# 122-token chunks, 32-bit transposes, Q in token order, one store per block, and a new job order in a convolution + token-mixing kernel

## The chip, the core and the metric

The kernel runs on one core of one Trainium2 chip. The metric is the device time of one execution in microseconds (us), taken several times; medians with the range are given. Every ratio between two kernels is the mean time of one kernel's fast runs over the mean time of the other's fast runs of the same rounds, so it is not quite the ratio of the medians quoted beside it. A run is "slow" when it is more than 1.5% above the fastest of its kernel. A profiled execution has a span of its own; it lies about 1.5 to 2 us under the timed figure of the same run.

In the profile, PE is the matmul engine, PEld its weight loads, DVE the vector engine, ACT the scalar engine, POOL the third compute engine (here it mostly issues the loads of x), and SP the engine that issues weight loads and output stores. "L640" is a line of that kernel's source.

## The reference

Eight batches of 4224 tokens with 192 features. A depthwise causal convolution over 7 taps with softmaxed weights per head, then a linear token mixer, a ReLU, and an output projection:

```python
# x: (8, 4224, 192) float32, weight: (8 heads, 7 taps), w_q/w_k: (192, 64), w_out: (192, 192)
w = softmax(weight)                                   # over the taps
out = einsum('hk,bskhg->bshg', w, windows of 7 tokens of x)   # y
# mixer
wq = y @ w_q
wk = y @ w_k
W_tok = (1/sqrt(64)) * einsum('bsd,btd->bst', wq, wk)
mixed = einsum('bst,btd->bsd', W_tok, y)
return (maximum(mixed, 0) @ w_out).astype(float32)
```

There is no softmax in the mixer, so `mixed = wq @ (wk.T @ y)`, and `wk.T @ y` is `w_k.T @ (y.T @ y)`. Both kernels use this. They form G = y.T y (192x192), then M = w_k.T G, then Z = relu(M.T q) and O = Z w_out, with two half sequences side by side in the 128 rows.

## The kernel before

Each batch goes through these jobs. **Y** is the convolution: a matmul with a band matrix over chunks of tokens, evacuated to bf16. **T** is the DVE transpose of y in 32x32 blocks. **Q** is the matmul of the transposed y with w_q. **G** accumulates y.T y, and **M** follows from it. **Z** and **O** follow, then the stores. A greedy list scheduler in the kernel source places all jobs in one order per engine, before anything runs. It takes each job's priority from `KEYS` and each duration from a small model.

```python
KEYS = {   # job kind: (start, length) in batches; priority of a job
    "Y": (-0.27, 0.38), "T": (0.24, 1.17), "Q": (0.01, 0.95), "G": (0.03, 0.98),
    "Z": (0.61, 1.2), "O": (1.24, 0.87),
}
CW, NCK = 120, 18           # 18 chunks of 120 tokens for each half; a chunk's load has 126 rows
...
# T: 6 transposes a batch, each of 128 x 1152 bf16 elements
(YB[:, g, c : c + 3, :].rearrange("p c d -> p (c d)"),
 Y[:, b % 2, 3 * k : 3 * k + 3, :].rearrange("p c d -> p (c d)"))
...
# Q: moving operand contiguous, output in a chunk-wise order that needs small extra casts
rhs = YB[r, g, :, 32 * blk : 32 * blk + 32]
...
# O: stores, each half of a block apart; q == 1 is the block's second part
for h in range(2):
    if rem:                                            # the last 64 tokens of each half
        parts = [(0, 64, row(h, 17 * CW), [[D, 64], [1, D]])]
    elif i < 3:
        parts = [(0, 128, row(h, 32 * i), [[CW * D, 16]] + chunk)]
    else:
        parts = [(0, 96, ...), (96, 126, ...), (126, 128, ...)]
    for p0, p1, at, dims in parts:
        st = P.dma("sp", lambda e, ...: e.dma_start(bass.AP(out_t, at, dims), src), og[orr], evs)
...
# POOL: batch 0 is loaded first; then the w_k and w_out casts, which wait for their weights;
# only after them the loads of batches 1 to 7, six batch buffers in all
```

## Time and profile before

| quantity | value | where it is read |
|---|---|---|
| time | 187.51 us (187.36 to 187.66, 3 runs) | timing |
| span of the profiled run | 185.6 us | page |
| first band matmul (job Y) | 13.70 us | timeline of PE |
| first Q matmul of batch 0 / batch 1 | 22.90 / 38.77 us | starts of L466 |
| period in the middle | 38.6 us for two batches, 19.3 each | starts of L466: 59.01 and 97.59 |
| transposes | 48, 62.6 us of DVE | groups |
| last compute / end | 174.7 / 185.6 us | timeline |

The first fence is from the page of the kernel before: the span in 40 slices of 4.64 us. Digits are tenths (9 is 90% or more); "PEclk" is the granted matmul clock; "DMA" is the mean busy share of the 16 DMA engines, and the last row is what they moved.

```profile
span 185.6 us, 4685 instructions
...
PE   7907977998998999979989999799899999799500
...
PEclk9995799999999999999999999999999999999965
DMA  3997999999999999999999999968634860588894
GB/s 58 139 200 81 119 186 186 190 184 209 279 332 282 250 252 315 280 188 274 325 309 206 263 309 308 177 199 302 193 100 126 263 206 15 170 266 253 272 313 129
```

PE is near full in the middle but falls to 7 or 8 tenths again and again, every three to five slices, so about twice in the 38.6 us of two batches. The clock is at half in the fourth slice (0.50 from 15 to 20 us), after PE had been idle in the third (busy for 1.30 us from 10 to 15 us). The DMA engines are full until about 120 us, except in the fourth slice (81 GB/s): POOL's casts had waited for the w_out weights until 13.6 us, and the loads of batch 1 stand behind these casts, the first issued at 17.0 us.

Two groups of the kernel before (line, engine, operation, output<-input, shapes, count | busy us, mean ns of one | idle before):

```profile
L780 DVE STREAM_TRANSPOSE yb<-y 128x1152 bf16<-128x1152 bf16 x48 | 62.6, 1349 | 0.4
...
L466 PE MATMUL ps<-yb,wq 32*64 32x288 bf16 x768 | 15.1, 285 | 1.2 <-DVE zt L787 0.6
```

A transpose of 1152 16-bit elements takes 1.30 us of DVE when they run back to back (62.6 us for 48; the mean of 1349 ns counts their overlap), six times a batch.

A stretch of the chain of work that ended last (start us, us, what), kernel before, one batch in the middle:

```profile
71.21 0.38 PE ps L403 x2
71.59 0.67 DVE zt L787
72.26 3.80 DVE yb L780 x3
76.09 0.32 DVE y L812
76.45 0.69 DVE zt L787
77.17 3.90 DVE yb L780 x3
81.07 0.59 DVE zt L787
```

Two runs of three transposes in a row, 3.8 and 3.9 us, stand in the chain here, with single evacuations between them. In this stretch the chain is on the vector engine, not on PE. Over 60 to 100 us, DVE transposes are 19.3% of the chain.

Windows of the middle, kernel before (stretch, its length, then busy us and count of PE, PEld, DVE, ACT and POOL, granted clock, DMA share, GB/s; the DMA share sums the packets' times over 16 engines and can pass 1 where packets overlap):

```profile
60.00:80.00 20.00, 19.77 (x260) 14.23 (x260) 17.43 (x28) 17.90 (x36) 5.50 (x7) 1.00 1.36 268
80.00:100.00 20.00, 18.30 (x234) 12.14 (x231) 17.37 (x31) 16.89 (x33) 0.00 (x0) 1.00 1.36 269
```

PE counts as busy for 38.1 of 40 us. Ends of matmuls are modelled, so this says less than it seems to: the prediction worked out from the columns that a batch needs 17.0 of its 19.3 us. (Its 2.4 GHz is what the trace of the changed kernel shows at full clock: matmuls start 82 ns apart with 192 columns and 215 ns apart with 512, so 320 more columns take 133 ns, 2.4 a nanosecond.)

### The profile page before, as it was taken

How to read it: one execution, taken by the hardware profiler on the slowest of the kernel's cores; microseconds unless marked ns; L12 is line 12 of the kernel's file. 1: busy time of each engine (PE TensorE's matmuls, PEld its weight loads, DVE VectorE, ACT ScalarE, POOL GpSimd, SP SyncE). 2: the span in 40 equal slices, each digit the busy share in tenths (PEclk: the TensorE clock that was granted, in tenths of full speed). 3: DMA queues.
4: the chain of work that ended last, by engine and by line, in shares of the span. 5: the costliest groups of instructions: out<-in, count | busy, mean ns of one | idle time of the engine just before them, and what ended most of it. 6: DMA issues, size and time to landing. Idle time of an engine off the chain costs nothing.

```text
span 185.6 us, 4685 instructions
## 1 busy us (share of the span) xinstructions
PE 158.1 (85%) x1934; PEld 105.7 (57%) x1934; DVE 141.1 (76%) x239; ACT 136.5 (74%) x261; POOL 49.2 (27%) x74
## 2 busy tenths in 40 slices
PE   7907977998998999979989999799899999799500
PEld 2303663576556765857477758574578567657300
DVE  4846786998699779985998689968995899767100
ACT  2114739985998789868997899769986998599600
POOL 6808999999207226000000000000000000000000
PEclk9995799999999999999999999999999999999965
DMA  3997999999999999999999999968634860588894
GB/s 58 139 200 81 119 186 186 190 184 209 279 332 282 250 252 315 280 188 274 325 309 206 263 309 308 177 199 302 193 100 126 263 206 15 170 266 253 272 313 129
DMA packets 53589, 40.39 MB, mean 218 GB/s; under 512 B 44096, under 2 KB 45376, under 8 KB 53568
## 3 DMA queue, kind: packets, MB, share of 16 engines
q0 software_dynamic: 41216, 13.64, 63.3%
q1 hardware_dynamic: 12352, 26.45, 43.9%
q8 instruction: 15, 0.25, 0.5%
q14 instruction: 6, 0.05, 0.1%
HBM read 27.73 MB, written 25.95 MB: 289 GB/s over the span
## 4 chain that ended last, share of the span: by engine, by line
PE 42%; DVE 25%; ACT 18%; DMA 6%; issue 2%; POOL 1%; ACTq 0%
DVE yb L780 19%; PE ps L623 9%; PE ps L403 7%; PE ps L625 7%; PE ps L466 6%; DMA xw<-in_x_dram 6%; ACT o_sb L782 6%; ACT zt L785 5%; ACT y L782 5%; PE ps L586 3%; DVE zt L787 3%; PE ps L517 2%; PE ps L518 2%; PE ps L601 2%; ACT qt L782 2%
## 5 line engine op out<-in xcount | busy, mean ns | idle before, releaser
L780 DVE STREAM_TRANSPOSE yb<-y 128x1152 bf16<-128x1152 bf16 x48 | 62.6, 1349 | 0.4
L782 ACT COPY o_sb<-ps 128x768 f32<-128x768 f32 (+1 forms) x66 | 51.7, 800 | 9.0 <-PE ps L625 4.8
L782 ACT CAST y<-ps 128x864 bf16<-128x864 f32 (+3 forms) x80 | 43.1, 631 | 7.3 <-PE ps L403 7.2
L623 PE MATMUL ps<-wall,zt 128*128 128x192 bf16 x272 | 45.5, 249 | 2.4 <-ACT y L782 1.4
L625 PE MATMUL ps<-wall,zt 128*128 128x384 bf16 x136 | 44.3, 326 | 0.0
L403 PE MATMUL ps<-xw,band 126*128 126x432 bf16 x128 | 33.2, 367 | 4.9 <-DMA xw<-in_x_dram 4.6
L205 POOL DMA_DIRECT2D xw<-in_x_dram x32 | 32.1, 1008 | 17.4 <-issue 17.4
L623 PEld LDWEIGHTS ps<-wall,zt 128*128 128x128 bf16 x272 | 26.5, 114 | 15.7 <-ACT y L782 4.4
L517 PE MATMUL ps<-y 128*128 128x192 bf16 x144 | 33.8, 248 | 1.2 <-DVE y L782 1.2
L518 PE MATMUL ps<-y 128*128 128x192 bf16 x144 | 33.7, 248 | 0.0
L787 DVE TENSOR_SCALAR zt<-ps 128x512 bf16<-128x512 f32 (+1 forms) x61 | 30.2, 522 | 4.1 <-PE ps L586 2.0
L785 ACT ACTIVATE zt<-ps 128x512 bf16<-128x512 f32 (+1 forms) x59 | 33.1, 609 | 0.0
L519 PE MATMUL ps<-y 128*128 128x128 bf16 x144 | 31.7, 220 | 0.0
L586 PE MATMUL ps<-qt,m_sb 128*128 128x512 bf16 (+1 forms) x80 | 25.6, 343 | 0.4 <-ACT qt L782 0.4
L782 ACT CAST qt<-ps 128x64 bf16<-128x64 f32 (+4 forms) x43 | 14.3, 400 | 11.9 <-PE ps L466 11.6
L782 DVE CAST y<-ps 128x864 bf16<-128x864 f32 x16 | 16.8, 1057 | 4.3 <-PE ps L403 3.6
L403 PEld LDWEIGHTS ps<-xw,band 126*128 126x128 bf16 x128 | 10.7, 102 | 15.9 <-issue 8.8
L518 PEld LDWEIGHTS ps<-y 128*128 128x128 bf16 x144 | 14.2, 99 | 5.2 <-issue 0.2
L517 PEld LDWEIGHTS ps<-y 128*128 128x128 bf16 x144 | 14.2, 98 | 4.9 <-DVE y L782 1.9
L601 PE MATMUL ps<-qt,m_sb 128*128 128x512 bf16 (+1 forms) x40 | 13.8, 344 | 3.6 <-DVE zt L787 3.1
L466 PE MATMUL ps<-yb,wq 32*64 32x288 bf16 x768 | 15.1, 285 | 1.2 <-DVE zt L787 0.6
L625 PEld LDWEIGHTS ps<-wall,zt 128*128 128x128 bf16 x136 | 15.3, 112 | 0.0
(64 smaller groups left out, 121.5 us busy)
## 6 DMA issues: line engine op xcount, KB each, us to landing
out_dram<-o_sb SPq DMA_DIRECT2D x48, 384.0 KB
xw<-in_x_dram POOLq DMA_DIRECT2D x24, 378.0 KB, 22.5
out_dram<-o_sb SPq DMA_DIRECT2D x16, 288.0 KB
xw<-in_x_dram POOLq DMA_DIRECT2D x8, 425.2 KB, 22.7
out_dram<-o_sb SPq DMA_DIRECT2D x16, 90.0 KB
out_dram<-o_sb SPq DMA_DIRECT2D x16, 48.0 KB
xw<-in_x_dram POOLq DMA_DIRECT2D x16, 29.2 KB, 26.6
xw<-in_x_dram POOLq DMA_DIRECT2D x8, 45.0 KB, 16.9
```

The costliest lines, as they stand in the source:

```text
L205: return e.dma_start(XW[0:rows, b % NX, slot : slot + n, :], bass.AP(x_t, base, [[D, rows], [CW * D, n], [1, D]]),)
L403: last = e.matmul(PS[:, k + j, 0:432], BAND[0 : 6 + CW, h, :], rhs, start=True, stop=True)
L517: e.matmul(PS[:, 7, 0:192], y[:, 0:128], y[:, 0:192], start=c == 0, **fl)
L518: e.matmul(PS[:, 7, 192:384], y[:, 256:384], y[:, 192:384], start=False, **fl)
L519: return e.matmul(PS[:, 7, 384:512], y[:, 128:256], y[:, 128:256], start=False, **fl)
L586: return e.matmul(PS[:, bk, 0:w], M_SB[:, b % 2, 256 * h : 256 * h + 128], QT[:, b % 2, s0 : s0 + w], start=True, stop=True)
L623: e.matmul(o[:, 192 * h : 192 * h + 192], ZT[:, zr, h, cols], WO1, start=h == 0, stop=False, **kw)
L625: last = e.matmul(o[:, 0:384], ZT[:, zr, 2, cols], WO2, start=False, stop=True, **kw)
L780: last = e.transpose(o, i)
L782: last = e.copy(o, i) if eng == "act" else e.tensor_copy(o, i)
L785: last = e.activation(o, i, AF.Relu)
L787: last = e.tensor_scalar(o, i, 0.0, None, op0=ALU.max)
```

## The change

Its intent, part by part:

1. Transposes of 32-bit pairs: two bf16 features are moved as one int32, so each of the 48 transposes has 576 elements instead of 1152. The Q matmul picks the even or odd features by a step of two.
2. Q in token order: each chunk's output goes straight to its token place, and the small casts go.
3. One store per block (both halves), so 40 stores; the last two full blocks are stored in two parts each. The remainder of 64 tokens of each half becomes one store; the kernel before had two of 64 rows.
4. Chunks of 122 tokens in loads of 128 rows; batch 0 in four groups, the first without waiting for a memset; the w_k and w_out loads wait for batch 0's second group; the weight casts are moved from POOL to DVE and ACT.
5. A recalibrated model and new priorities for the job order, and redundant semaphore waits are removed.

```diff
 KEYS = {
-    "Y": (-0.27, 0.38), "T": (0.24, 1.17), "Q": (0.01, 0.95), "G": (0.03, 0.98),
-    "Z": (0.61, 1.2), "O": (1.24, 0.87),
+    "Y": (-1.0, 0.64), "Q": (-0.3, 1.4), "G": (0.06, 0.63), "Z": (0.73, 1.5), "O": (1.59, 0.9),
 }
+CLOCK = {
+    "x0": (5.0, 6.6, 9.2, 11.6), "band": 6.5, "wq": 6.5, "wk": 11.0, "wo": 12.0, "x": (12.0, 12.0),
+    "store": 5.0, "now": 0.05, "hold": 1.5,
+}
...  (removal of redundant waits cut)
-    CW = 120
+    CW = 122
...
+    GROUPS = [[(0, 3), (3, 9), (9, 15), (15, 18)]] + [[(0, 9), (9, 18)]] * (B - 1)
...
     for s, (src, wd) in enumerate(((wk_t, DH), (wo_t, D))):
-        wload(2 * s, 0, 128, src, 0, wd, wl[s + 1])
+        wload(2 * s, 0, 128, src, 0, wd, wl[s + 1], [xg[0][1]])
...  (band matrix set-up, casts of the weights cut)
             return [(
-                YB[:, g, c : c + 3, :].rearrange("p c d -> p (c d)"),
-                Y[:, b % 2, 3 * k : 3 * k + 3, :].rearrange("p c d -> p (c d)"),
+                YB[:, g, c : c + 3, :].rearrange("p c d -> p (c d)").bitcast(I32),
+                Y[:, b % 2, 3 * k : 3 * k + 3, :].rearrange("p c d -> p (c d)").bitcast(I32),
             )]
...
-                        blk = j if h == 0 else (8 + j if j < 4 else 2 + j)
-                        rhs = YB[r, g, :, 32 * blk : 32 * blk + 32]
+                        c = 64 * ((0, 1, 2), (4, 5, 3))[h][j // 2] + j % 2
+                        rhs = YB[r, g, :, c : c + 63 : 2]
...  (Z and M jobs cut)
-            for h in range(2):
-                if rem:
-                    parts = [(0, 64, row(h, 17 * CW), [[D, 64], [1, D]])]
-                elif i < 3:
...
+            at = (b * S + 512 * i) * D
+            if rem:
+                src, dims = OUT[:, orr, 0, 0:D], [[HALF * D, 2], [D, 64], [1, D]]
+            elif tail:                                 # tail = b == B - 1 and i >= 2
+                at += 2 * q * D
+                src = OUT[:, orr, :, 2 * D * q : 2 * D * q + 2 * D]
+                dims = [[4 * D, 128], [HALF * D, 2], [1, 2 * D]]
+            else:
+                src = OUT[:, orr, :, :]
+                dims = [[4 * D, 128], [HALF * D, 2], [1, 4 * D]]
+            st = P.dma(
+                "sp", lambda e: e.dma_start(bass.AP(out_t, at, dims), src), og[orr], evs,
+            )
...  (the scheduler's cost model cut)
```

## The prediction

> **What bounds the kernel now.** 187.5 us timed, 185.6 us in the profile.
> - Head: the chain of waits has the first band matmul at 13.7 us, released by the landing of batch 0's first loads (issued by 3.3 us). The band matrix itself was ready at 9.9 us (timeline).
> - Middle: the chain repeats every two batches in 38.6 us, so 19.3 us per batch. Matmul columns at 2.4 GHz need 17.0 us of that; 2.4 us are stalls. They sit where PE waits for DVE and ACT results. DVE carries six transposes of 1.30 us per batch (62.6 us in all, 19% of the chain), and the two evacuating engines together about 33.5 us per batch, 87% of their time.
> - Tail: the last compute ends at 174.7 us. SP still issues stores until 183.3 us (23 issues in 18.9 us, 0.8 us each); 11 us follow the last matmuls.
>
> **Costs of the change.**
> 1. Transposes: 576 elements of 32 bits instead of 1152 of 16. The trace shows 1.04 ns per element plus about 0.1. [...]I estimate 0.65-0.7 us: -3.8 us of DVE per batch.
> 2. Q in token order: the small casts (8 to 64 columns, 0.15-0.22 us each) go; about -0.6 us of evacuation. Evacuation falls to some 29 us per batch, 14.5 per engine. Risk: Q's moving operand now has a step of two elements.
> 3. PE columns hardly change: an estimate of 137.5 us for the whole program, 17.2 us per batch with array-mode switches. PE becomes the limit of the middle. I expect 17.5-18 us per batch: about -11 us over the middle.
> 4. Head: the first load waits for no memset, three chunks land first, the shift chain shrinks (five predicated copies 2.75 us -> about 1.3). First band matmul near 7.5-8.5 us, -5.5 us. PE ran at half clock from 15 to 20 us (windows) after its idle gap; that penalty should also go. Some 5 us of idle stay while batch 0 lands and its chain Y-G-M fills.
> 5. Stores: 112 issues become 40[...]; the last two blocks are stored in halves. Bytes are the same. The last two batches of output come in about 19 us of PE time, 6.5 MB, near the 293-333 GB/s that stores alone reached, so a backlog of 1-2 MB stays: tail 4-6 us, saving about 6.
> 6. Loads: pure x loads ran at 187 GB/s written; row count falls 2%. Together loads and stores need about 17.5 us per batch when mixed. So DMA is close behind PE, and some waits for x are possible.
>
> **Sum.** 8 + 137.5 + 10 stalls (fill, drain, middle) + 5 tail = 160.5 in the profile, plus 1.9 = about 163 us. Range 156 to 172. Faster 0.97, same 0.02, slower 0.01.
>
> **What would show it.** Right: transposes 0.65-0.7 us; first band matmul before 9 us; batch period 17.2-18 us; DVE and ACT under 85% busy mid-run; last compute by 157, span end within 6 us of it; granted clock never 0.5 after the start. Wrong in step 1: transposes above 1 us; step 2: Q's 48 matmuls above 0.95 us; step 4: first matmul still released by the load or later than 10 us; step 5: SP issues until well past the last compute; step 6: PE waits released by x landings after 40 us.
>
> **What would make it wrong.** The job order comes from a model: engines work in order, so one mis-modelled time stalls PE each batch. DMA saturation: output starts later and faster, and stores of the remainder in [2,64,192] form may run on few engines.

The sum: 160.5 us in the profile and 163 us timed. What its steps take from the trace of the kernel before:

- Step 1: DVE casts of 512 and 864 elements took 691 and 1057 ns (medians), 1.04 ns per element, and a transpose of 1152 elements at 1.30 us is that plus about 0.1 us. That a 32-bit element takes no longer than a 16-bit one was the assumption: this trace has only 16-bit transposes.
- Step 3, the array-mode switches: in the middle (55 to 100 us) the start of a 128*128 matmul of 128 columns is followed by the next start after 55 ns, and after 149 to 170 ns when the next is one of Q's 32*64 matmuls.
- Step 6: the 17.5 us are the estimate. It fits the trace: 40.39 MB over eight batches are 5.05 MB a batch, which take 17.5 us at 289 GB/s, and the trace has 285 GB/s from 70 to 80 us and 290 from 90 to 100.

## The result and the profile after

The changed kernel took **177.91 us** (median of 4 runs, 177.14 to 179.23) against 187.58 us (187.36 to 188.32, 4 runs) of the kernel before. The ratio of the fast runs is 0.950 (95% interval 0.945 to 0.956). It is faster by 5%. The predicted 163 us and the range of 156 to 172 us missed it. The profiled run below (span 177.5 us) is the 179.23 us run, the longest of the four, and counts as fast.

The same rows of the page, kernel after, slices of 4.44 us:

```profile
PE   7739869999999999999999999999599999999300
...
PEclk9965978999999999999999999999969999999975
DMA  3999999999999999999999999555640585497980
GB/s 57 130 170 189 206 189 192 190 194 190 261 285 293 262 213 335 250 327 213 329 248 331 216 333 304 199 187 198 219 178 11 215 317 187 158 392 230 388 292 23
```

Three things are new. PE is at 9 tenths in every slice from the 7th to the 28th, without the dips of before. In slice 29 (124 to 129 us) it falls to half, and the clock follows in slice 30. The DMA engines have been at half since slice 26 (111 us), and in slice 31 they move 11 GB/s. So the hole falls in a time when the DMA engines are not full. (The 11 GB/s come after it and are not its sign: the kernel before has a slice of 15 GB/s, and e1 below one of 22.) At the end PE has nothing to do in the last two slices, and in the very last the DMA engines move only 23 GB/s.

The group of transposes after:

```profile
L787 DVE STREAM_TRANSPOSE yb<-y 128x576 int32<-128x576 int32 x48 | 33.8, 749 | 2.7 <-ACT y L795 2.7
```

The transposes cost 33.8 us, not 62.6. Back to back one takes 0.70 us (33.8 us for 48), so step 1 of the prediction held.

Windows of the middle, and of the stretch with the hole, kernel after, columns as before:

```profile
60.00:80.00 20.00, 19.63 (x257) 14.44 (x258) 13.57 (x27) 18.84 (x32) 0.00 (x0) 1.00 1.30 288
80.00:100.00 20.00, 19.59 (x255) 14.29 (x257) 14.88 (x29) 18.73 (x34) 0.00 (x0) 1.00 1.34 274
120.00:130.00 10.00, 7.56 (x116) 5.13 (x122) 6.58 (x14) 7.42 (x13) 0.00 (x0) 1.00 0.65 232
130.00:140.00 10.00, 9.69 (x116) 7.06 (x102) 5.34 (x10) 7.74 (x16) 0.00 (x0) 0.83 0.17 62
```

PE has 39.2 of 40 us in the middle. From 120 to 130 us it has only 7.6 of 10, and from 130 to 140 us the clock is 0.83. The chain over 60 to 100 us is now PE work almost throughout. The period is 17.83 to 17.95 us per batch (Q starts at 66.75, 84.70, 102.53 and 120.38 us), inside the predicted 17.5 to 18.

The chain at the hole, kernel after:

```profile
126.59 0.69 DVE zt L793
127.28 1.36 DVE yb L787 x2
128.73 0.53 PE ps L433 x2
```

and the waits of PE after 36 us, kernel after (what waited <- for what: us in total, times, longest):

```profile
PE ps L433 <- DVE yb L787: 2.2, 1, 2.2
```

The profile puts the hole down to a transpose, which is an inference: a wait for several semaphores is given to the one that came last. In the trace, L433 waits for two, one of DVE and one of the last x load. PE's sequencer passed the wait for x at 128.63 to 128.68 us and started the matmul at 128.73. The transpose that ended at 128.63 is simply next on an engine that kept working. That the load is the cause is shown by its landing, here, and by e1, e2 and e4 below. Its semaphore counts one update for each of 16 DMA engines and each of its DMAs, and this is when the last ten of the 48 updates came (us from the start of the span):

```
last load of x (batch 7, second half): kernel after
110.1 110.3 111.0 111.2 | 120.1 125.3 126.9 127.2 128.3 128.6
```

Forty-two updates had come by 111.2 us. Six, so two engines times three DMAs, came 9 to 17 us later. The x queue as a whole shows the same: it moved 58.8 GB/s from 105 to 110 us, then 9.8, 8.9, 5.9 and 7.9 GB/s in the next four stretches of 5 us, with about one row in flight on average.

The tail, kernel before and then kernel after:

```profile
175.00:186.00 11.00, 0.00 (x0) 0.00 (x0) 0.00 (x0) 0.00 (x0) 0.00 (x0) 0.63 0.70 229
```

```profile
165.00:170.00 5.00, 0.68 (x7) 0.36 (x4) 0.36 (x1) 1.40 (x2) 0.00 (x0) 1.00 1.03 383
170.00:178.00 8.00, 0.00 (x0) 0.00 (x0) 0.00 (x0) 0.00 (x0) 0.00 (x0) 0.56 0.33 110
```

Last compute ended at 166.4 us and the span at 177.5, an 11.1 us tail, where the prediction had 5. After 170 us only 110 GB/s moved, at a third of the DMA engines' time. The store completions in the trace show which part is late. The last part of the last full block has 14 engines done by 172.5 us and its last two updates at 173.7 and 174.8; the remainder store, issued at 169.1 us, has one update at 170.7 and its last two at 176.6 and 177.0 us, when nothing else was left.

The head, kernel after (timeline of PE: start, us, engine, line and operation, count, [idle before <-releaser]):

```profile
8.58 0.55 PE L433 MATMUL ps<-xw,band 128*128 128x144 bf16 x6 [1.10 <-ACT band L371]
9.86 0.30 PE L433 MATMUL ps<-xw,band 128*128 128x144 bf16 x2 [0.73 <-ACT y L789]
12.36 1.60 PE L433 MATMUL ps<-xw,band 128*128 128x288 bf16 x6 [2.20 <-DMA xw<-in_x_dram]
```

The first band matmul starts at 8.58 us, released by the band matrix and not by the load, as predicted. But PE then waits 2.2 us for batch 0's second group, the clock is 0.55 from 10 to 15 us, and another wait of 2.0 us follows at 21.6 us, where the casts of w_out wait for weights that landed only at 21.9 us:

```profile
ACT wo L789 <- DMA wst<-in_moe_w_out_dram: 1.7, 1, 1.7
```

### The profile page after: what moved, and what is told of

It is laid out like the page before. It is cut to its first block, busy times and chain, and to the rows that moved or that the text cites. A ratio compares the mean times of both kernels' runs of the same rounds, so it can differ in the third digit from the quotient of the medians.

```text
span 177.5 us, 4686 instructions
## 1 busy us (share of the span) xinstructions
PE 152.8 (86%) x1958; PEld 112.8 (64%) x1980; DVE 113.1 (64%) x228; ACT 138.1 (78%) x255; POOL 47.6 (27%) x71
## 3 DMA queue, kind: packets, MB, share of 16 engines
HBM read 27.77 MB, written 25.95 MB: 303 GB/s over the span
## 4 chain that ended last, share of the span: by engine, by line
PE 71%; DMA 8%; ACT 7%; issue 3%; POOL 2%; SPq 1%; DVE 1%; ACTq 0%; POOLq 0%
PE ps L640 13%; PE ps L433 11%; PE ps L642 11%; PE ps L597 9%; PE ps L498 8%; PE ps L526 7%; PE ps L527 6%; DMA xw<-in_x_dram 4%; DMA wst<-in_moe_w_out_dram 4%; PE ps L528 4%; POOL xw L252 2%; ACT qt L789 2%; ACT y L789 2%; SPq L310 1%; ACT o_sb L789 1%
## 5 line engine op out<-in xcount | busy, mean ns | idle before, releaser
L789 ACT CAST y<-ps 128x864 bf16<-128x864 f32 (+7 forms) x94 | 50.7, 596 | 8.2 <-PE ps L433 7.9
L793 DVE TENSOR_SCALAR zt<-ps 128x512 bf16<-128x512 f32 x54 | 36.8, 683 | 21.6 <-PE ps L597 19.5
L433 PE MATMUL ps<-xw,band 128*128 128x432 bf16 (+2 forms) x144 | 36.1, 354 | 8.6 <-ACT y L789 2.9
L640 PE MATMUL ps<-wo,zt 128*128 128x192 bf16 x256 | 42.5, 248 | 0.3
L642 PE MATMUL ps<-wo,zt 128*128 128x384 bf16 x128 | 41.8, 326 | 0.0
L787 DVE STREAM_TRANSPOSE yb<-y 128x576 int32<-128x576 int32 x48 | 33.8, 749 | 2.7 <-ACT y L795 2.7
L640 PEld LDWEIGHTS ps<-wo,zt 128*128 128x128 bf16 x256 | 26.2, 115 | 11.5 <-ACT o_sb L789 3.6
L597 PE MATMUL ps<-qt,m_sb 128*128 128x512 bf16 x74 | 26.1, 380 | 1.1 <-issue 1.0
L792 ACT ACTIVATE zt<-ps 128x512 bf16<-128x512 f32 x42 | 24.4, 620 | 0.3 <-PE ps L597 0.3
L433 PEld LDWEIGHTS ps<-xw,band 128*128 128x128 bf16 x144 | 12.3, 104 | 16.4 <-ACT y L789 4.6
L527 PEld LDWEIGHTS ps<-y 128*128 128x128 bf16 x144 | 14.6, 101 | 8.4 <-issue 0.7
L526 PEld LDWEIGHTS ps<-y 128*128 128x128 bf16 x144 | 14.6, 102 | 5.4 <-issue 1.1
L528 PEld LDWEIGHTS ps<-y 128*128 128x128 bf16 x144 | 14.5, 101 | 0.1
```

Of the source, the lines that this page charges most:

```text
L433: last = e.matmul(PS[:, k + j, 0 : 48 * n], BAND[:, h, :], rhs, start=True, stop=True)
L526: e.matmul(PS[:, 7, 0:192], y[:, 0:128], y[:, 0:192], start=c == 0, **fl)
L527: e.matmul(PS[:, 7, 192:384], y[:, 256:384], y[:, 192:384], start=False, **fl)
L528: return e.matmul(PS[:, 7, 384:512], y[:, 128:256], y[:, 128:256], start=False, **fl)
L597: return e.matmul(PS[:, bk, :], m[:, parts[k] : parts[k] + 128], q, start=True, stop=True)
L640: e.matmul(o[:, 192 * h : 192 * h + 192], z[:, h, cols], WO1[:, :], start=h == 0, stop=False, **kw)
```

## The experiments

Each line of the table is one kernel. e1, e2 and e4 are the changed kernel with one edit, e3 has the edits of e1 and e2, and e5 to e10 have e3 as their base. The kernel before took 186.87, 187.33 and 187.06 us in the three sets of runs, so ratios are the safer comparison across sets.

| kernel | edit | time, us (range) | ratio to before (95%) |
|---|---|---|---|
| after | the change | 177.91 (177.14 to 179.23) | 0.950 (0.945 to 0.956) |
| e1_rem16 | remainder store as two DMAs of 64 rows | 169.97 (168.63 to 171.43, one slow) | 0.907 (0.900 to 0.915) |
| e2_wearly | w_k, w_out loads don't wait for x | 177.06 (176.41 to 177.80) | 0.948 (0.942 to 0.953) |
| e3_both | both | 168.02 (167.47 to 168.13) | 0.898 (0.893 to 0.903) |
| e4_rem1 | remainder store in 61 + 3 rows | 191.07 the fast one of two runs | none |
| e5_t16 | e3, 16-bit transposes again | 180.01 (178.96 to 182.58, one slow) | 0.960 (0.956 to 0.964) |
| e6_oldkeys | e3, priorities of before | 177.68 (177.13 to 179.10) | 0.951 (0.947 to 0.955) |
| e7_warm | e3, dummy matmuls in the head | 168.79 (168.25 to 169.97) | 0.902 (0.899 to 0.906) |
| e8_pool | e3, weight casts back on POOL | 169.69 (169.19 to 171.20) | 0.908 (0.905 to 0.911) |
| e3_again | e3 once more | 167.99 (167.61 to 168.73) | 0.896 (0.890 to 0.903) |
| e9_whole | e3, last blocks stored whole | 168.35 (167.87 to 168.62) | 0.898 (0.893 to 0.904) |
| e10_pool_tail | e3, half of the last stores on POOL | 169.27 (168.62 to 169.75) | 0.903 (0.897 to 0.910) |

### e1_rem16: is the remainder store the two late engines?

The theory: the remainder store's destination has the shape [2, 64, 192], and only 2 of the 16 DMA engines carry it. In the trace of the changed kernel such a store gives its semaphore 3 updates (issued at 74.8 us: one at 75.8, two at 85.5), where the store of a full block gives 16. The rival is that the loads and stores together have no bandwidth left. The edit splits the same bytes into two stores of 64 rows, as the kernel before had them.

```diff
-            st = P.dma("sp", lambda e: e.dma_start(bass.AP(out_t, at, dims), src), og[orr], evs)
+            if rem:
+                for h in range(2):
+                    st = P.dma("sp", lambda e, h=h: e.dma_start(
+                        bass.AP(out_t, at + h * HALF * D, [[D, 64], [1, D]]),
+                        OUT[64 * h : 64 * h + 64, orr, 0, 0:D]), og[orr], evs)
+            else:
+                st = ...   # as before
```

> The changed kernel with one edit: the remainder store of each batch, one DMA whose output side is [2, 64, 192], becomes two DMAs of 64 rows. Theory A (the [2,64,192] store puts all of its 128 rows on two DMA engines, whose share of the loads then falls behind): the late pairs of landing updates vanish, the last load lands near 112 us instead of 128.6, the 2.3 us wait of the band matmul at 126 us and the half clock after it go, the tail after the last compute falls from 11.8 to about 8 us; time 169 to 172 us against 177.9. Theory B (loads and stores together saturate all DMA engines): bytes are the same, so the last load still lands near 128 us and the time stays within 1 us of 177.9.

The median of 169.97 us includes a slow run. The fast runs have a mean of 169.53 us, 8.5 us less than the changed kernel's 178.05. The last x landing moved from 128.6 to 117.1 us (112 was expected), and after 36 us PE waits for 0.3 us in all:

```profile
PE ps L600 <- ACT zt L803: 0.3, 1, 0.3
```

The end of the span came 6.3 us after the last compute (160.4 and 166.7 us) instead of 11.1. The bytes are unchanged, so the rival falls: it was not a lack of total bandwidth. The trace also counts the engines. A store of a full block gives its semaphore 16 updates, the [2, 64, 192] store only 3 (one early, two when its data land), and each 64-row store of e1 16.

### e4_rem1: the opposite direction

If the count of engines is the cause, one engine must be worse than two. Each half's store is cut into 61 rows and 3 rows; that the 61 rows then fall on one engine was the expectation, to be tested by this run.

```diff
+                for h, r0, r1 in ((0, 0, 61), (0, 61, 64), (1, 0, 61), (1, 61, 64)):
+                    ... bass.AP(out_t, at + (h * HALF + r0) * D, [[D, r1 - r0], [1, D]]) ...
```

> The changed kernel with the remainder store split into 61 + 3 rows per half, so that by theory A most of its rows fall on one engine instead of two: twice the extra work on that engine. A: one late landing update per load instead of two, the last load lands near 140 to 150 us, and the time rises to 188 us or more. B: as before, 178 us within 1.5 us. If the number of engines is not set by the row count in this way, the time stays or falls.

The fast run took 191.07 us, 13 us more than the changed kernel (the other run, 197.92 us, is slow, so this rests on one run). The semaphores fit: a 61-row and a 3-row store give 6 updates together, where two of 64 rows give 32. That these are 1 + 1 and 1 + 3 is the reading. The count of store issues is not the cause: e1 has two a batch and is faster than the changed kernel with one, e4 has four and is slower. The last x load had one straggler for each of its DMAs in place of two: its updates ended 107.8, 109.1 | 135.4, 137.7, 138.0 us. Its x queue crept at 2.5 to 5.5 GB/s from 110 to 140 us, less than the two engines' 5.9 to 9.8. PE now waits for x openly:

```profile
PE ps L433 <- DMA xw<-in_x_dram: 8.9, 3, 4.2
PE ps L433 <- DVE yb L798: 1.5, 1, 1.5
```

The issue lines of the last x load tell the same in one number (the last column is us from issue to landing), for after, e1 and e4 in that order:

```profile
xw<-in_x_dram POOLq DMA_DIRECT2D x1, 33.0 KB, 72.2
```

```profile
xw<-in_x_dram POOLq DMA_DIRECT2D x1, 33.0 KB, 58.5
```

```profile
xw<-in_x_dram POOLq DMA_DIRECT2D x1, 33.0 KB, 80.2
```

The size of the delay can be estimated from the trace. One remainder store has 128 rows of 768 bytes, so with two engines each carries 64 of them instead of 8. By 128 us four of them had been issued and had landed (issued at 56.6, 74.8, 92.8 and 110.6 us), 224 extra rows for each of the two engines. The trace has 49 ns for such a row (median), so the estimate is 11 us; the landing was late by 11.5 us against e1. For one engine that carries 122 rows a batch the same sum gives about 22 us, and e4's landing was late by 21 (138.0 against 117.1 us). So the stores load two engines with more bytes than the others, and the last x load and the last full block's store, which are spread over all 16, waited for these two (128.6 against 111.2 us, and 174.8 against 172.5).

### e2_wearly and e3_both: the head

The w_k and w_out loads are issued at once, not after batch 0's second group.

```diff
-        wload(2 * s, 0, 128, src, 0, wd, wl[s + 1], [xg[0][1]])
+        wload(2 * s, 0, 128, src, 0, wd, wl[s + 1], ())
```

> The changed kernel with one edit: the loads of the key and output weights no longer wait for the second group of batch 0. Theory C (the wait of ACT for the output weights, until 21.9 us, stalls PE 2.2 us and brings half clock until 28 us): these weights land before 12 us, that gap goes and PE reaches batch 1's work 2.5 to 4 us earlier. But if theory A holds, the late last load at 128 us takes most of it back, and the time falls by 0 to 2 us only. Theory D (the head is bound by the landing of batch 0, whose last rows come at 16.7 us): the gap moves, and PE's start on batch 1 comes no more than 1 us earlier.

> Both edits of the two runs before. If A and C both hold: 2.5 to 4 us below the first of them, 166 to 168.5 us, last compute near 157 us. If D holds instead of C: equal to the first within 1 us.

w_k and w_out landed at 7.4 and 12.8 us instead of 18.3 and 21.9, and in the window of 20 to 25 us PE was busy 4.22 us where it had been 2.97. Alone this gave 0.9 us at most (177.06 us; the ranges overlap, so it may be nothing): the last x still landed at 128.6 us. PE now lost its time earlier, between 100 and 120 us (16.8 of 20 us busy), and there the profile names x. Waits of PE after 36 us, e2:

```profile
PE ps L433 <- DMA xw<-in_x_dram: 3.2, 1, 3.2
```

So the gain in the head was lost again in the wait for x. With the remainder store mended as well (e3), the time is 168.02 us. Fast runs against fast runs that is 1.6 us below e1, where 2.5 to 4 were expected; the times don't overlap (at most 168.13, at least 168.63), but the intervals of the ratios do. This is the best kernel, 10% below the kernel before. The repeat in another set (e3_again, told below) gave 167.99 us.

The same stretch as above in e3, windows of 120 to 140 us, and its end:

```profile
120.00:130.00 10.00, 10.00 (x129) 7.30 (x127) 6.19 (x11) 9.74 (x19) 0.00 (x0) 1.00 0.47 170
130.00:140.00 10.00, 9.96 (x135) 7.38 (x134) 7.30 (x17) 8.73 (x15) 0.00 (x0) 1.00 0.62 236
```

```profile
155.00:160.00 5.00, 3.90 (x36) 2.84 (x34) 2.38 (x6) 4.39 (x6) 0.00 (x0) 1.00 0.98 364
160.00:167.00 7.00, 0.00 (x0) 0.00 (x0) 0.00 (x0) 0.00 (x0) 0.00 (x0) 0.80 0.71 247
```

PE is full where the changed kernel had its hole, the clock is full, and the bytes are moved by 166.1 us. The starts of the Q matmuls give the account of the whole difference in these profiled runs between after (span 177.5) and e3 (span 166.1), 11.4 us:

```
                              after     e3_both   after later by
second Q of batch 0           27.96      25.22    2.7   (w_out wait in the head)
first Q of batch 6           120.38     117.68    2.7   (the middle is the same)
first Q of batch 7           142.16     135.52    6.6   (+3.9: late x)
last compute                 166.4      159.8     6.6
end of the span              177.5      166.1    11.4   (+4.8: late stores)
```

### e5_t16 and e6_oldkeys: where the 10% comes from

Both undo one part of the change on top of e3: e5 goes back to 16-bit transposes with contiguous Q operands, e6 to the old priorities.

```diff
# e5_t16 (and the old layout of w_q)
-                YB[:, g, c : c + 3, :].rearrange("p c d -> p (c d)").bitcast(I32),
-                Y[:, b % 2, 3 * k : 3 * k + 3, :].rearrange("p c d -> p (c d)").bitcast(I32),
+                YB[:, g, c : c + 3, :].rearrange("p c d -> p (c d)"),
+                Y[:, b % 2, 3 * k : 3 * k + 3, :].rearrange("p c d -> p (c d)"),
-            evacs=[(make, ("TD", b, k), 576, "transpose")],
+            evacs=[(make, ("TD", b, k), 1152, "transpose")],
# e6_oldkeys
-    "Y": (-1.0, 0.64), "Q": (-0.3, 1.4), "G": (0.06, 0.63), "Z": (0.73, 1.5), "O": (1.59, 0.9),
+    "Y": (-0.27, 0.38), "Q": (0.01, 0.95), "G": (0.03, 0.98), "Z": (0.61, 1.2), "O": (1.24, 0.87),
```

> The kernel with both earlier edits (168.0 us), but with the old transposes: 1152 elements of 16 bits, Q reading contiguous blocks, the query weights laid out as before; all else as it is, and the job order made with the longer transposes. Theory E (the transposes, with the evacuations on DVE and ACT, held the old middle at 19.3 us per batch): DVE gets about 3.6 us more per batch, both evacuating engines come near 95% busy, the batch period rises from 17.85 us to 18.5 to 19.3 us, time 174 to 181 us. Theory F (PE alone sets the period, DVE had room): period at most 18.1 us, time at most 170 us.

> The same base with the order keys of the kernel before (convolution of the next batch 0.27 of a batch ahead instead of a whole batch; the measured durations in the model kept). Theory G (the long look-ahead is what hides the chain from convolution to Q): PE waits come back, period over 18.4 us, time 172 to 178 us. Rival: the greedy order with measured durations is enough whatever the keys, time within 1.5 us of 168.0.

With 16-bit transposes the ratio is 0.960 against 0.898, about 12 us of the gain; with the old priorities it is 0.951, about 10 us. Both times are as expected (174 to 181 and 172 to 178 us). Each part alone takes back about half or more of the 19 us, so the gains don't add: together they would pass the whole. A reading that fits is that the short transposes pay most when the order lets PE run ahead of them, and the order when the evacuating engines have room, but no run undoes both, so this is not shown. The middle of e6 and of e3, windows as before:

```profile
60.00:80.00 20.00, 18.03 (x248) 13.41 (x249) 12.51 (x21) 18.17 (x37) 1.34 (x2) 1.00 1.35 271
80.00:100.00 20.00, 18.94 (x253) 14.12 (x255) 12.67 (x21) 18.61 (x39) 0.00 (x0) 1.00 1.34 274
```

```profile
60.00:80.00 20.00, 19.89 (x259) 14.30 (x258) 14.64 (x30) 18.86 (x34) 0.00 (x0) 1.00 1.34 272
80.00:100.00 20.00, 19.78 (x272) 14.43 (x277) 14.07 (x31) 18.51 (x32) 0.00 (x0) 1.00 1.35 273
```

In e6 PE was busy 18.0 and 18.9 of 20 us from 60 to 100 us, against 19.9 and 19.8 in e3. For e5 only a slow run was profiled, so its profile is not used for sizes.

### e7_warm and e8_pool: the half clock and the casts in the head

In the changed kernel the matmul clock fell to half at 10.5, 24.1 and 129.9 us (it was 0.55 on average from 10 to 15 us), and in the 3.4 us before each fall PE had been idle for 2.0 to 2.2 us. e7 adds 8 warm-up matmuls and 36 dummies behind batch 0's first group. e8 puts the eight weight casts back on POOL, behind the loads of batches 1 and 2.

```diff
# e7_warm
-        for i in range(60):
+        for i in range(68):
...
+        if job.name == ("Y", 0, 0, 3):
+            P.op("pe", again, [z_warm])        # again: 36 matmuls of 128 x 128 into bank 7
# e8_pool
+    load_batch(1)
+    load_batch(2)
+    for name, o, i, z, grp in (...):           # the eight casts
+        cast = pool(lambda e, o=o, i=i: e.tensor_copy(o, i), [grp, cast] + z)
```

> The same base with 8 more warming matmuls at the start and 36 between the first convolution group and the second, where PE waits for the load. Theory H (the half clock from 12 to 17 us costs time): the granted clock stays at full, PE starts batch 1 earlier by 1 to 1.5 us, time 166.5 to 167.2 us. Rival: the landing of batch 1 (21.8 and 26.1 us) binds there, time within 0.5 us of 168.0.

> The same base with the eight casts of the key and output weights moved from ACT and DVE to POOL, after it has issued the loads of batches 1 and 2. Theory I (these 2.5 us of ACT work ahead of batch 0's evacuations delay the head): PE gap at 21 to 24 us shrinks, time 166 to 167 us. Rival: the landing of batch 1 binds, time within 0.5 us of 168.0.

Neither gained anything, and neither came out as its theory or its rival had it. e7 took 168.79 us and e8 169.69 us, 0.8 and 1.7 us more than e3. e7 raised the mean clock from 12.4 to 20 us (0.79 instead of 0.67), but it moved the half clock instead of removing it: e3 has it from 10.6 to 17.5 us, e7 from 16.8 to 20.3, after PE had waited 2.0 us for batch 0's third group. The first Q of batch 0 then came at 21.39 us, where e3 has 20.35, and 0.7 us of this was still there at batch 7 (136.21 against 135.52). So e7 doesn't tell what the half clock costs. The landing of batch 1 (21.7 and 26.0 us for its two groups) moved in neither run, but that it ends the fill of the pipeline is not shown. Why e8 is slower stays open; its job order differs too.

### e9_whole, e10_pool_tail, and e3 again as the control: is the tail SP's issuing?

In the changed kernel SP's last half-block stores took about 1.2 us each to issue, so the tail might be SP. e9 stores the last blocks whole; e10 lets POOL issue the second part of each.

```diff
# e9_whole
-        tail = b == B - 1 and i >= 2
+        tail = False
# e10_pool_tail (a semaphore of its own for the two stores)
-                    "sp", lambda e: e.dma_start(bass.AP(out_t, at, dims), src), og[orr], evs,
+                    "pool" if tail and q == 1 else "sp",
+                    lambda e: e.dma_start(bass.AP(out_t, at, dims), src),
+                    og2 if tail and q == 1 else og[orr], evs,
```

> The version with both mends once more, as the control of the two runs beside it: 168 us, 0.898 of before.

> Both mends, and the last two full blocks of the last batch stored whole (one store each, 768 KB) instead of in two halves. Theory J, as the prediction has it (halves let the last bytes leave sooner): whole stores start later and the end moves back by 1 to 2 us, to about 169.5 us. Rival K (each half store of 1.5 KB rows takes as long to issue as a whole one, 1.2 us, so that halving only doubles the issue work of SP while the queue is full): same or up to 1 us faster, 167 to 168 us, with fewer SP issues after the last compute.

> Both mends, and the second half of each of the last two full blocks issued by POOL, which is idle then, instead of SP. Theory K (SP's issues set the tail of 6.3 us): the last landing comes 1 to 2 us earlier, about 166.5 us, span end within 5 us of the last compute. Rival L (the tail is the backlog of bytes at the rate of the stores, 360 to 380 GB/s in the last slices): no gain, 168 us within 0.5, or slightly slower.

e9 took 168.35 us against 167.99 of the control, the same within the error: the halves were worth at most some tenths, and SP's issues are not the limit. e10 was 1.3 us slower: from 160 to 165 us it moved 348 GB/s where the control moved 366, and it ended at 167.8 us. In the control the DMA engines are full from 150 to 165 us (share 0.96 and 1.03) at 364 to 366 GB/s. So the remaining tail of some 6.3 us is the backlog of output bytes at that rate, and not the issuing.

## Why the prediction was wrong

The direction was right and most mechanisms were; the size was not. The prediction's sum was "8 + 137.5 + 10 stalls (fill, drain, middle) + 5 tail = 160.5" in the profile; measured was 177.5. Of the 17.0 us between them, 6.1 lie in the tail (11.1 for 5), 3.9 in the hole before batch 7, 2.7 in the wait for w_out, 0.6 in the first matmul and 3.7 in the rest of the work of PE. e3 is without the hole, the wait and 4.8 of the tail.

- **Step 5 failed, and it is the main cause.** "Bytes are the same" was taken to mean the same cost. The remainder stores are 3% of the output (0.79 of 25.95 MB), but in their [2, 64, 192] form they ran on two engines. Sharing those engines with the loads made the last x late (the 3.9 us hole, which the "10 stalls" didn't have) and left a store queue on two engines at the end: a tail of 11.1 us for the term "5". e1 undid only this, gained 8.5 us and came inside the predicted range; e4 made it worse by 13. The prediction named this risk in its last lines and put no number on it. Given the count of engines, the number follows from the sum shown under e4: 56 rows more on each of two engines in every batch, when the prediction itself had DMA close behind PE. The count is read from the trace of the changed kernel (3 updates for such a store, 16 for a full block), and e1 and e4 agree with it in both directions.
- **Step 6** allowed for "some waits for x", and put them down to total bandwidth. The wait came, at 126 to 129 us, but in a stretch where 14 of 16 engines had no more x to bring. The loads of 128 rows gave hardly more rate either: 187 to 190 GB/s against 180 to 187 before, in stretches of 5 us from 25 to 40 us.
- **Step 4** was half right. The first band matmul came at 8.58 us (predicted 7.5 to 8.5), released by the band matrix. The "5 us of idle" and "half-clock penalty should also go" were wrong: the first Q of batch 0 came only 2.6 us earlier than before (20.29 for 22.90), with the clock at 0.55. The w_out loads queued behind x cost another 2.7 us that the prediction missed, and e3 shows it. What the half clock cost is open, since e7 only moved it.
- **Steps 1 to 3 held.** Transposes 0.70 us back to back (predicted 0.65 to 0.7). The bytes are the same and the time is nearly half: 576 elements fewer take 0.60 us less, 1.04 ns each. Q's matmuls with the step of two showed next to no penalty: 285 ns each on average in the kernel before, 294 in the changed kernel, whose clock was low for longer, and 285 in e3. The prediction's threshold of 0.95 us for 48 of them was too tight to tell anything: they took 0.94 us in the kernel before and 0.95 to 0.98 in the changed kernel (1.58 once, at half clock). The period was 17.85 us, predicted 17.5 to 18. One sign that it named failed: ACT was to be under 85% busy, and it was busy for 18.8 of 20 us (94%) from 60 to 80 us, while DVE had 13.6. The total of the two is near the predicted 29 us a batch, but not split evenly.
- **The tail term** of 5 was right in kind where nothing else interfered: e3 has 6.3 us, and e9 and e10 show it to be backlog, as the prediction had it.
- **With the two mends** the kernel takes 168.0 us, inside the predicted range, 5 us over the predicted 163: last compute at 159.8 where the sum has 155.5, and 1.3 us more of tail. So the prediction described a kernel that the change nearly was.

## What to carry to other kernels

Before counting a DMA by its bytes, look in the trace at how many updates it gives its semaphore: here a small store with 3 updates in place of 16, on two of 16 engines, delayed loads and stores that are spread over all of them (the last x by 11.5 us), and it showed up as a late landing elsewhere, with the DMA engines half idle. When a merge of DMAs cuts their number, check the updates of the merged DMA again: here two stores of 64 rows gave 16 each, and their merge in the form [2, 64, 192] gave 3. When two mends sit in series (here the head and the late x), test them together as well, because the first alone may only move its gain into the second wait.

## What the runs show of the hardware

- Stores on few engines: with the [2, 64, 192] store the last x load had two late engines, with 61 rows one, with 64 rows none. 3% of the stored bytes on two engines cost 8.5 us of 178, and on one engine about 21.5 us (191.07, a single run, against 169.53).
- Loads of x, which cast float32 to bf16 in rows of 384 written bytes, ran at 180 to 187 GB/s of written bytes with 126 rows and at 187 to 190 with 128 (kernel before and kernel after, stretches of 5 us from 25 to 40 us).
- A transpose takes 0.70 us for 128x576 32-bit and 1.30 us for 128x1152 16-bit elements, back to back.
- The matmul clock: in the traces of the kernels before and after it fell to half four times before the last compute, at 14.0 us (before) and at 10.5, 24.1 and 129.9 us (after). In the 3.41 us up to each fall PE had been idle for 3.09, 2.16, 2.03 and 2.17 us in all (ends of matmuls are modelled), never throughout. The stretches at one clock, but for those cut off by the start and the end, lasted 6.83 and 157.0 us (before) and 6.83, 6.83, 3.41, 102.4, 3.41 and 37.5 us (after), multiples of 3.41 us. Cut into pieces of 3.41 us, they have pieces with up to 1.82 us of idle time after which the clock stayed full.
